# Attention, Fourier mixing and two MLPs: the first chunk's layer norm moved into attention

## The chip, the cores and the metric

The kernel runs on one core of a Trainium2 chip. The metric is the device time of one execution in microseconds (us), lower is better. TensorE is called PE below, VectorE DVE, ScalarE ACT, GpSimd POOL and SyncE SP, as in the profile's rows.

## What is computed

The reference chains three blocks on float32 data. Batch is 4, with 8 heads, a sequence of 576 and a head size of 64, so the model width is 512.

```python
def _attn_ref(q, k, v):
    scores = scale * np.matmul(q, k.transpose(0, 1, 3, 2))
    mask_local = (rel >= 0) & (rel < stride)
    mask_strided = (rel >= 0) & (pos[None, :] % stride == pos[:, None] % stride)
    ...
    attn = softmax(np.where(mask, scores, -1e9))
    return np.matmul(attn, v)

def _moe_ref(x, w_ch1, w_ch2):
    X = np.fft.fft(np.fft.fft(x, axis=1), axis=2)
    u = x + np.real(X)
    un = (u - mean(u)) / np.sqrt(var(u) + 1e-06)
    return u + np.maximum(un @ w_ch1, 0.0) @ w_ch2

def _moe2_ref(x, w_tok1, w_tok2, w_ch1, w_ch2):
    h = np.maximum(x.transpose(0, 2, 1) @ w_tok1, 0.0) @ w_tok2
    u = x + h.transpose(0, 2, 1)
    return u + np.maximum(u @ w_ch1, 0.0) @ w_ch2
```

Half of the heads use the local mask, half the strided one. The change touches the layer norm in the middle of the second block (`un`), for the first 384 of its 2304 rows.

## The kernel before, in words

**Attention.** There are 24 groups, six for each batch element b: three of local heads (kind "l") and three of strided heads (kind "s"). Groups are numbered 0 to 23 by `gno` in the main loop. A group has two halves e = 0 and 1. For each half PE makes the scores `sc` (mask first, then keys), DVE takes a row maximum (`TENSOR_REDUCE st<-sc`), ACT makes four exps `sm<-sc` with their sums, PE transposes them (`tp<-sm`), ACT copies the transposes (`pt<-tp`), PE multiplies with the values (`av<-pt`), and DVE scales (`x<-av`). SP writes `x` to the DRAM tensor `xd[b]`.

**Fourier mixing.** Two or three groups later the Fourier transform of a finished batch element is laid in slices between the groups: SP loads `xa` and `xr` from `xd`, DVE makes `w` and `e`, ACT and POOL split `e` into a high and a low part `f`, PE makes five products `g` in banks of the PSUM tag "m" (two of them), ACT and DVE copy each bank out as `gh` and `gl`, PE makes `fa` and `fb`, and DVE adds the result to `xa` and `xr`, which SP writes to `ud[b]`. The fourth batch element's transform comes after attention, beside the first MLP.

**Layer norm and first MLP.** Rows of `ud` are loaded back as tiles `u` of 128 rows (three tiles are one chunk of 384 rows, called u0, u1, u2 for the first chunk, u3 to u5 for the second). `ln_stats` (lines 452 to 463) takes BN_STATS and BN_AGGR on DVE, a Sqrt on ACT (line 459) and a reciprocal on DVE (line 460), `ln_apply` (lines 465 to 468) makes `lm` on ACT, `Mlp.transposes` (lines 390 to 401) transposes it on PE to `ut` and splits it into `uth` (ACT) and `utl` (DVE). `gemm1` and `gemm2` then run over 16 column blocks, with the products `h` and `oo`.

In the main loop the first chunk is loaded at group 19, its statistics are asked for at group 23 behind the reduce of group 21, and `lm` and the transposes follow after the loop (lines 582 to 606).

**What sets the order.** Tile frees and waits are found by the framework, which also reorders each engine's instructions by a timeline of its own before the program is built. Each engine then runs its list strictly in that order, and SP issues its DMAs in that order, waiting in place for what a DMA depends on. `behind(ins, prev)` asks that `ins` stand behind `prev` in the order, without a wait on the chip. Pools are stacks of memory: the pool "mlp" (`dp`) is opened where "attn" (`ap`) was closed, so that its first tiles overlie `vs`, `qz0`, `qz1`.

Of the kernel before, what the change touches and what calls it, by code (L numbers as in the profile page):

```python
# [9 lines left out]
F32 = mybir.dt.float32  # L10
F32R = mybir.dt.float32r
I32 = mybir.dt.int32
U32 = mybir.dt.uint32
AF = mybir.ActivationFunctionType
ALU = mybir.AluOpType
AX = mybir.AxisListType

B, H, S, D = 4, 8, 576, 64
DM = 512
P = 128  # L20
# [10 lines left out]
SR = [18 * c for c in SC]  # L31


E_MIN = float(np.array(1024 << 20, np.int32).view(np.float32))
E_MAX = float(np.array(1279 << 20, np.int32).view(np.float32))

# [6 lines left out]
def attention_fourier_mlp_kernel(ctx: ExitStack, tc: tile.TileContext, a: dict, out: bass.AP):  # L43
    nc = tc.nc
# [118 lines left out]
    k_t, qz = {}, []  # L163
# [221 lines left out]
    class Mlp:  # L385
# [3 lines left out]

        def transposes(self, c, i, src):  # L390
            if i == 0:
                self.uT[c] = (self.pool.tile([P, 4, 384], F32R, tag="uth", name="uth", bufs=2),
                              self.pool.tile([P, 4, 384], F32R, tag="utl", name="utl", bufs=2))
            th, tl = self.uT[c]
            tp = (ps_o if c < self.split else ps_m)("ut")
            for kd in range(4):
                nc.tensor.transpose(tp[:, kd * P:(kd + 1) * P], src[:, kd * P:(kd + 1) * P], ident)
            tv = tp.rearrange("p (k t) -> p k t", k=4)
            s = slice(i * P, (i + 1) * P)
            nc.scalar.activation(out=th[:, :, s], in_=tv, func=AF.Copy)  # L400
            nc.vector.tensor_tensor(out=tl[:, :, s], in0=tv, in1=f32(th[:, :, s]), op=ALU.subtract)
# [46 lines left out]
    def ln_load(T, mlp):  # L448
        u = mlp.u[T // 3, T % 3] = mlp.u_tile(T // 3)
        return u_rows(T, u)  # L450

    def ln_stats(us, pool, prev=None):
        n = len(us)
        mv = pool.tile([P, 3, 4], F32, tag="mv", name="mv", bufs=2)
        for i, u in enumerate(us):
            st = pool.tile([P, 6], F32, tag="bs", name="bs", bufs=2)
            behind(nc.vector.bn_stats(out=st, in_=u), prev)
            nc.vector.bn_aggr(out=mv[:, i, 0:2], in_=st)
        behind(nc.scalar.activation(out=mv[:, :n, 2], in_=mv[:, :n, 1], func=AF.Sqrt, bias=eps), gl[-1].exp)
        nc.vector.reciprocal(out=mv[:, :n, 3], in_=mv[:, :n, 2])  # L460
        nc.vector.scalar_tensor_tensor(out=mv[:, :n, 2], in0=mv[:, :n, 0], scalar=-1.0, in1=mv[:, :n, 3],
                                       op0=ALU.mult, op1=ALU.mult)
        return [mv[:, i] for i in range(n)]

    def ln_apply(u, mv, pool):
        m = pool.tile([P, DM], F32, tag="lm", name="lm", bufs=2)
        nc.scalar.activation(out=m, in_=u, func=AF.Identity, scale=mv[:, 3:4], bias=mv[:, 2:3])
        return m

    def ln(u, pool):  # L470
# [2 lines left out]
    if True:  # L473
# [14 lines left out]
        nc.vector.memset(eps, 1e-6)  # L488
        nc.scalar.activation(out=warm, in_=eps, func=AF.Exp)
        v_t["s"] = ap.tile([126, 5, 256], F32, name="vs")  # L490
        for g in range(2):
            qz.append(ap.tile([P, 2, 2, S], F32, name=f"qz{g}"))
        v_t["l"] = ap.tile([P, 6, 256], F32, name="vl")
        load_qk(0, 0, ap)
        for g in range(2):
# [59 lines left out]
        def group(g, e, nm):  # L555
            return getattr(gl[min(g, len(gl) - 1)], nm)[e if g < len(gl) else 1]

        slices = []

        for gno, g in enumerate(gl):  # L560
            b, gi = g.b, g.gi
            if gi == 3 and b + 1 < B:
                load_qk(b + 1, 0, ap)
                load_vl(b + 1)
            if gi == 0 and b > 0:
                load_qk(b, 1, ap)
                load_vs(b)
            g.scores()
            for e in range(2):
                g.softmax(e)  # L570
            for e in range(2):
                g.trans(e)
            for e in range(2):
                g.av(e)
                g.out(e)
            if gi == 2 and b > 0:
                for i in range(3):
                    four[b - 1].load(i)
                slices += fft(b - 1)
            while slices and slices[0][0] <= gno:  # L580
                slices.pop(0)[1]()
            if gno == 19:
                us = [u_rows(T, lp.tile([P, DM], F32, tag="u", name="u", bufs=6)) for T in range(3)]
            if gno == 23:
                mvs = ln_stats(us, lp, gl[21].red[1])
            if gno == 9:
                hold[0] = four[0].last
            if gno >= 2 and (gno - 2) % 3 == 0:
                advance()
                load_wa()  # L590
# [12 lines left out]
        for T in range(3):  # L603
            m1.u[0, T] = us[T]
        for T in range(3):
            m1.transposes(0, T, ln_apply(us[T], mvs[T], lp))
        fk["mlp"] = dp
        for i in range(3):
            four[3].load(i)
# [62 lines left out]
        def c_load(b, ts):  # L672
            for t in ts:
# [6 lines left out]
                else:  # L680
                    r = m1.u_tile(0)
                    if t % 3 == 0:
                        for nm in ("uth", "utl"):
                            xbuf[nm] = dp.tile([P, 3, DM], F32R, tag=nm, name=nm, bufs=2)
                    h, l = xbuf["uth"][:, t % 3], xbuf["utl"][:, t % 3]
                q = slice(q0, q0 + n)
                nc.sync.dma_start(out=r[q], in_=x2d[p][j, q, :])
                nc.scalar.activation(out=h[q], in_=r[q], func=AF.Copy)
# [43 lines left out]
        def c1(b):  # L732
# [11 lines left out]
            for m in range(2):  # L744
                if b == 1:
                    if m == 0:
                        th, tl = (dp.tile([P, 3, DM], F32R, tag=nm, name=nm, bufs=2) for nm in ("uth", "utl"))
                    hh, hl = th[:, m], tl[:, m]
                elif b > 1:
                    hh, hl = (wa.tile([P, DM], F32R, tag="wa", name=nm) for nm in ("hh", "hl"))  # L750
                else:
# [432 lines left out]
```

## Time and profile before

| | us |
|---|---|
| median of 3 runs | 936.71 |
| lowest and highest | 935.81, 942.67 |
| the profiled execution | 935.66 |
| its span, first to last instruction | 933.9 |
| PE busy in it | 900.8 (96%) |
| DVE, ACT, POOL busy | 551.6, 411.5, 322.7 |

The profiled execution's own time is 1.76 us longer than its span. Times in rows count from the start of the span. Attention runs to about 149 us; the first MLP starts at about 150 us. Mean granted clock of PE in the execution is 0.99 of 2.4 GHz.

### The profile page before, as it was taken

What the parts mean: (1) busy time and instruction counts of PE and PEld (TensorE: products, weight loads), DVE (VectorE), ACT (ScalarE), POOL (GpSimd) and SP (SyncE); (2) the same over time, 40 slices, a digit from 0 to 9 for tenths busy, and PEclk for the clock granted to TensorE, in tenths of its full rate; (3) what the DMA queues carried; (4) which work ended last, traced back from release to release, by engine and by line L of the source; (5) the groups of instructions that cost most, each with busy time, mean ns of one, the idle gap of its engine ahead of it and who ended that gap; (6) DMA issues with size and microseconds to landing.
All of it is one profiled execution on the core that took longest, in us unless ns stands there. A gap on an engine that the chain in (4) does not pass through costs nothing.

```text
span 933.9 us, 15390 instructions
## 1 busy us (share of the span) xinstructions
PE 900.8 (96%) x5554; PEld 831.1 (89%) x5554; DVE 551.6 (59%) x1022; ACT 411.5 (44%) x1073; POOL 322.7 (35%) x378
## 2 busy tenths in 40 slices
PE   6979998999999999999999998999999999999997
PEld 5869997999899889888888987777899999999997
DVE  4758876988884433444443444735534444888774
ACT  4978768453342234233323333323445445454432
POOL 2402202333320143344444345622223001946660
PEclk9889999999999999999999999999999999999999
DMA  9988772434331254544754665588833287146351
GB/s 244 277 266 246 222 229 89 153 114 147 131 111 66 82 171 128 192 126 140 213 149 133 206 183 166 171 271 287 318 127 146 102 270 228 44 160 215 132 196 46
DMA packets 116915, 161.00 MB, mean 172 GB/s; under 512 B 9602, under 2 KB 70120, under 8 KB 116840
## 3 DMA queue, kind: packets, MB, share of 16 engines
q1 hardware_dynamic: 114872, 157.30, 53.4%
q0 software_dynamic: 1712, 2.51, 1.1%
q8 instruction: 44, 0.72, 0.3%
q14 instruction: 31, 0.25, 0.1%
q10 hardware_dynamic: 256, 0.21, 0.1%
HBM read 104.93 MB, written 55.06 MB: 171 GB/s over the span
## 4 chain that ended last, share of the span: by engine, by line
PE 56%; DMA 9%; DVE 7%; SPq 4%; ACT 3%; POOL 3%; issue 2%; DVEq 0%; ACTq 0%; POOLq 0%
PE oo L994 14%; PE oo L430 10%; PE h L411 10%; PE z L853 8%; PE y L853 4%; DMA wraw<-in_w1b_dram 4%; PE tk L742 3%; SPq L102 3%; PE tu L764 2%; PE w L853 2%; POOL wt L148 2%; DVE wu L113 2%; DMA wraw<-in_w2b_dram 2%; DVE wu L114 1%; ACT wu L107 1%
## 5 line engine op out<-in xcount | busy, mean ns | idle before, releaser
L994 PE MATMUL oo<-wo,ht 128*128 128x256 f32 x972 | 135.2, 281 | 0.0
L411 PE MATMUL h<-uth,wAh 128*128 128x384 f32 x384 | 130.0, 339 | 0.0
L411 PE MATMUL h<-uth,wAl 128*128 128x384 f32 x384 | 129.5, 337 | 0.0
L411 PE MATMUL h<-utl,wAh 128*128 128x384 f32 x384 | 129.5, 337 | 0.0
L994 PEld LDWEIGHTS oo<-wo,ht 128*128 128x128 f32 x972 | 127.5, 188 | 0.0
L430 PE MATMUL oo<-wAh,hh 128*128 128x512 f32 x288 | 114.0, 398 | 3.6 <-ACT hh L415 3.6
L430 PE MATMUL oo<-wAl,hh 128*128 128x512 f32 x288 | 113.6, 395 | 0.0
L430 PE MATMUL oo<-wAh,hl 128*128 128x512 f32 x288 | 104.8, 396 | 2.9 <-DVE hl L416 2.8
L416 DVE SCALAR_TENSOR_TENSOR hl<-h,hh 128x384 fp32r<-128x384 f32 x96 | 52.6, 552 | 78.4 <-ACT hh L415 78.4
L125 POOL TENSOR_TENSOR wAl<-wu,wAh 128x512 fp32r<-128x512 f32 x32 | 46.0, 1441 | 94.5 <-ACT wAh L124 90.5
L109 DVE TENSOR_SCALAR wu<-wu 128x512 f32<-128x512 f32 x56 | 29.4, 525 | 82.9 <-ACT wu L107 74.9
L148 POOL TENSOR_TENSOR wt<-wu 128x128 f32<-128x128 f32 x48 | 21.1, 460 | 161.0 <-DVE wu L114 157.8
L415 ACT ACTIVATE hh<-h 128x384 fp32r<-128x384 f32 x96 | 45.7, 484 | 67.3 <-PE h L411 67.2
L411 PEld LDWEIGHTS h<-uth,wAl 128*128 128x128 f32 x384 | 72.2, 188 | 3.0
L411 PEld LDWEIGHTS h<-utl,wAh 128*128 128x128 f32 x384 | 72.2, 188 | 2.1
L411 PEld LDWEIGHTS h<-uth,wAh 128*128 128x128 f32 x384 | 72.1, 188 | 2.2
L107 ACT ACTIVATE wu<-wraw 128x512 f32<-128x512 f32 (+1 forms) x62 | 40.8, 660 | 74.9 <-DMA wraw<-in_w1b_dram 45.7
L430 PEld LDWEIGHTS oo<-wAh,hl 128*128 128x128 f32 x288 | 53.8, 188 | 17.5 <-DVE hl L416 5.5
L430 PEld LDWEIGHTS oo<-wAh,hh 128*128 128x128 f32 x288 | 54.1, 188 | 14.7 <-ACT hh L415 5.2
L853 PE MATMUL z<-ut,wo 128*128 128x384 f32 x324 | 65.1, 340 | 1.4 <-DVE ut L821 1.4
L430 PEld LDWEIGHTS oo<-wAl,hh 128*128 128x128 f32 x288 | 54.1, 188 | 8.8
L229 ACT ACTIVATE sm<-sc,st 96x128 f32<-96x128 f32 (+2 forms) x176 | 61.3, 362 | 0.6
(198 smaller groups left out, 1966.6 us busy)
## 6 DMA issues: line engine op xcount, KB each, us to landing
wo<-wsd SPq DMA_DIRECT2D x84, 256.0 KB
wsd<-wbh SPq DMA_DIRECT2D x24, 448.0 KB
wsd<-wbl SPq DMA_DIRECT2D x24, 448.0 KB
u<-u2d SPq DMA_DIRECT2D x36, 256.0 KB
hd<-hs SPq DMA_DIRECT2D x12, 768.0 KB
hw<-hd SPq DMA_DIRECT2D x36, 256.0 KB
wraw<-in_w1a_dram SPq DMA_DIRECT2D x16, 512.0 KB
wraw<-in_w2a_dram SPq DMA_DIRECT2D x16, 512.0 KB
```

Source lines behind the costliest of these rows:

```text
L102: behind(nc.sync.dma_start(out=raw[:, n:n + w], in_=src.rearrange("p (c t) -> p c t", t=2)), hold[0])
L107: behind(nc.scalar.activation(out=f32(u), in_=f32(high), func=AF.Abs, scale=2.0**16), relu.get("hh"))
L109: clamp = eng().tensor_scalar(f32(u), f32(u), E_MIN, E_MAX, op0=ALU.max, op1=ALU.min)
L125: nc.gpsimd.tensor_tensor(out=lo[:, :n], in0=u, in1=f32(hi[:, :n]), op=ALU.subtract)
L148: nc.gpsimd.tensor_tensor(out=o, in0=x, in1=y, op=ALU.add if plus else ALU.subtract)
L229: self.exp = nc.scalar.activation(out=smv[:, j, :], in_=sc[:, j, :], func=AF.Exp, scale=SCALE, bias=st[:, 1, j:j + 1], accum_out=st[:, 2, ...
L411: nc.tensor.matmul(out=h[:, :384], lhsT=l[:, ws], rhs=r[:, kd, :], start=x == 0, stop=x == 11)
L415: relu["hh"] = nc.scalar.activation(out=hh, in_=h[:, :384], func=AF.Relu)
L416: relu["hl"] = nc.vector.scalar_tensor_tensor(out=hl, in0=h[:, :384], scalar=0.0, in1=f32(hh), op0=ALU.max, op1=ALU.subtract)
L430: nc.tensor.matmul(out=self.o[c][i], lhsT=l[:, s], rhs=r, start=first and x == 0, stop=last and x == 2)
L853: Unit.last = nc.tensor.matmul(out=bank[:, :384], lhsT=w[:, c + kd * P:c + kd * P + P], rhs=r[:, kd], start=first and x == 0, stop=x == 5, ...
L994: nc.tensor.matmul(out=acc[G][bank][:, 256 * half:256 * half + 256], lhsT=lh[:, i], rhs=w[:, c:c + 256], start=m == 0 and x == 0 and half ...
```

## The change

Five edits. The first chunk's rows are loaded at group 15 and not 19, and the statistics are asked for at group 17, behind that group's own reduce, and not at group 23. The statistics of several tiles at once take their inverse root by Newton's steps on DVE (`inverse_root`, a start value from the bits of the number, then three steps), and those of a single tile still by ACT's Sqrt. `lm` of u0 and u1 is made at groups 18 and 19, behind that group's last exp; that of u2 stays after the loop. The two buffers `qz0` and `qz1` are allocated in the other order. `uth` and `utl` become one tile `uT` with two halves, at each place that uses them.

```diff
+SEED = -0.67709067 * 2.0**-65
...
         def transposes(self, c, i, src):
             if i == 0:
-                self.uT[c] = (self.pool.tile([P, 4, 384], F32R, tag="uth", name="uth", bufs=2),
-                              self.pool.tile([P, 4, 384], F32R, tag="utl", name="utl", bufs=2))
+                t = self.pool.tile([P, 2, 4, 384], F32R, tag="ut", name="uT", bufs=2)
+                self.uT[c] = t[:, 0], t[:, 1]
...
+    def inverse_root(y, var, pool):
+        n = var.shape[1]
+        t = pool.tile([P, 2, 4], F32, tag="nr", name="nr", bufs=1)
+        v, z = t[:, 0, :n], t[:, 1, :n]
+        nc.vector.tensor_scalar_add(v, var, 1e-6)
+        nc.vector.tensor_scalar(z.bitcast(I32), v.bitcast(I32), 1, -1, op0=ALU.logical_shift_right, op1=ALU.bitwise_xor)
+        nc.vector.tensor_scalar_mul(y, z, SEED)
+        for _ in range(3):
+            nc.vector.scalar_tensor_tensor(out=z, in0=y, scalar=-0.5, in1=v, op0=ALU.mult, op1=ALU.mult)
+            nc.vector.tensor_tensor(out=z, in0=z, in1=y, op=ALU.mult)
+            nc.vector.scalar_tensor_tensor(out=y, in0=z, scalar=1.5, in1=y, op0=ALU.add, op1=ALU.mult)
...
-        behind(nc.scalar.activation(out=mv[:, :n, 2], in_=mv[:, :n, 1], func=AF.Sqrt, bias=eps), gl[-1].exp)
-        nc.vector.reciprocal(out=mv[:, :n, 3], in_=mv[:, :n, 2])
+        if n > 1:
+            inverse_root(mv[:, :n, 3], mv[:, :n, 1], pool)
+        else:
+            behind(nc.scalar.activation(out=mv[:, :n, 2], in_=mv[:, :n, 1], func=AF.Sqrt, bias=eps), gl[-1].exp)
+            nc.vector.reciprocal(out=mv[:, :n, 3], in_=mv[:, :n, 2])
...
-    def ln_apply(u, mv, pool):
+    def ln_apply(u, mv, pool, prev=None):
         m = pool.tile([P, DM], F32, tag="lm", name="lm", bufs=2)
-        nc.scalar.activation(out=m, in_=u, func=AF.Identity, scale=mv[:, 3:4], bias=mv[:, 2:3])
+        behind(nc.scalar.activation(out=m, in_=u, func=AF.Identity, scale=mv[:, 3:4], bias=mv[:, 2:3]), prev)
...
-        for g in range(2):
-            qz.append(ap.tile([P, 2, 2, S], F32, name=f"qz{g}"))
+        qz += [ap.tile([P, 2, 2, S], F32, name=f"qz{g}") for g in (1, 0)][::-1]
...
-            if gno == 19:
+            if gno == 15:
                 us = [u_rows(T, lp.tile([P, DM], F32, tag="u", name="u", bufs=6)) for T in range(3)]
-            if gno == 23:
-                mvs = ln_stats(us, lp, gl[21].red[1])
+            if gno == 17:
+                mvs = ln_stats(us, lp, g.red[1])
+            if 18 <= gno < 20:
+                ln1.append(ln_apply(us[gno - 18], mvs[gno - 18], lp, g.exp))
...
-            m1.transposes(0, T, ln_apply(us[T], mvs[T], lp))
+            m1.transposes(0, T, ln1[T] if T < 2 else ln_apply(us[T], mvs[T], lp))
```

Nothing is added to or taken from PE's, POOL's and SP's work; DVE has eleven instructions more, ACT one less. The order of the instructions is another on DVE, ACT and PE from about group 18 to the middle of the first MLP, and the same before and behind that. Three places, with the buffers' numbers behind the names:

On DVE, before, from the first reduce of group 18 (`st_1505<-sc_1492`) to the first reduce of group 19 (`st_1588`); `gl` copies a Fourier bank `g` out:

```order
L226 TENSOR_REDUCE st_1505<-sc_1492 96x4
L261 TENSOR_SCALAR st_1416<-st_1416 108x4
L262 RECIPROCAL st_1416<-st_1416 108x4
L263 TENSOR_TENSOR x_1383<-av_1374,st_1346 108x512
L342 TENSOR_TENSOR gl_1458<-g_1447,gh_1457 128x290
L226 TENSOR_REDUCE st_1505<-sc_1498 96x4
L342 TENSOR_TENSOR gl_1472<-g_1461,gh_1471 128x290
L226 TENSOR_REDUCE st_1588<-sc_1575 96x4
```

The same place in the changed kernel, where `st_1535` is group 18's, `u_1335` is u1 and `u_1337` is u2:

```order
L470 BN_STATS bs_1485<-u_1335 128x6
L471 BN_AGGR mv_1481<-bs_1482 128x2
L227 TENSOR_REDUCE st_1535<-sc_1522 96x4
L262 TENSOR_SCALAR st_1422<-st_1422 108x4
L471 BN_AGGR mv_1481<-bs_1485 128x2
L264 TENSOR_TENSOR x_1389<-av_1380,st_1352 108x512
L263 RECIPROCAL st_1422<-st_1422 108x4
L343 TENSOR_TENSOR gl_1464<-g_1453,gh_1463 128x290
L227 TENSOR_REDUCE st_1535<-sc_1528 96x4
L470 BN_STATS bs_1488<-u_1337 128x6
L343 TENSOR_TENSOR gl_1478<-g_1467,gh_1477 128x290
L264 TENSOR_TENSOR x_1447<-av_1442,st_1422 108x256
```

BN_STATS of u1 stands ahead of group 18's first reduce now, and that of u2 between its second reduce and the second `gl`; one BN_AGGR later comes group 19's first reduce, then Newton's steps, and BN_STATS of u3 ahead of the last of them.

On SP, before, the writes of the last rows of the first batch element to `ud0`, the queries and keys of the last batch element's strided heads, and the load of u2 (`u_1668`):

```order
L373 DMA ud0_73<-xr_713 33x512
L374 DMA ud0_73<-xa_712 32x512
L176 DMA qz1_137<-in_qt_dram 64x1152
L177 DMA k_1487<-in_kt_dram 128x1152
L445 DMA u_1668<-ud0_73 128x512
L276 DMA xd2_71<-x_1383 9x6x256
```

The same place in the changed kernel, with u2 as `u_1337`:

```order
L375 DMA ud0_73<-xa_712 32x512
L374 DMA ud0_73<-xr_713 33x512
L177 DMA qz1_136<-in_qt_dram 64x1152
L446 DMA u_1337<-ud0_73 128x512
L178 DMA k_1517<-in_kt_dram 128x1152
L277 DMA xd2_71<-x_1389 9x6x256
```

The two writes have changed places, and the load of u2 stands ahead of the keys' load and not behind it.

On ACT, before, from group 19's first exps (`sm_1587`) to the start of its second half (`st_1588<-st_1588`):

```order
L229 ACTIVATE sm_1587,st_1588<-sc_1575,st_1588 96x128 x4
L340 ACTIVATE gh_1557<-g_1547 128x290
L340 ACTIVATE gh_1571<-g_1561 128x290
L239 ACTIVATE pt_1531<-tp_1526 128x384
L239 ACTIVATE pt_1607<-tp_1602 128x384
L227 ACTIVATE st_1588<-st_1588 96x4
```

The same place in the changed kernel, where `lm_1605` is the layer norm of u0:

```order
L230 ACTIVATE sm_1619,st_1620<-sc_1607,st_1620 96x128 x3
L341 ACTIVATE gh_1587<-g_1577 128x290
L230 ACTIVATE sm_1619,st_1620<-sc_1607,st_1620 96x128
L240 ACTIVATE pt_1561<-tp_1556 128x384
L483 ACTIVATE lm_1605<-u_1333,mv_1481 128x512
L341 ACTIVATE gh_1601<-g_1591 128x290
L240 ACTIVATE pt_1639<-tp_1634 128x384
L228 ACTIVATE st_1620<-st_1620 96x4
```

`lm` of u0 stands ahead of a Fourier copy `gh`, of group 19's first `pt` and of its second half. The load of ACT's table for Sqrt stands behind the last exp of attention in both kernels, ahead of a Sqrt of three columns and one of a single column before, of one of a single column (u3's) now.

## Rows read from the trace of the kernel before

**Rows 1.** Stretches: length, busy (instructions) of PE, PEld, DVE, ACT, POOL; clock, DMA, GB/s.

```profile
116.00:126.00 10.00, 10.00 (x94) 9.55 (x93) 4.22 (x11) 7.61 (x38) 0.52 (x1) 1.00 0.75 243
126.00:140.00 14.00, 14.00 (x134) 13.74 (x132) 12.89 (x30) 8.99 (x40) 1.81 (x2) 1.00 0.68 224
140.00:150.00 10.00, 7.38 (x54) 5.67 (x53) 8.52 (x29) 9.06 (x38) 2.03 (x3) 1.00 0.21 60
```

**Rows 2.** Timeline of PE, 140 to 150 us.

```profile
140.56 1.30 PE L237 MATMUL tp<-ident_r,sm 108*108 108x108 f32 x4 [0.24 <-ACT sm L229]
...
148.18 0.97 PE L252 MATMUL av<-vs,pt 108*108 108x64 f32 x8 [1.43 <-ACT pt L239]
...
149.86 0.85 PE L332 MATMUL g<-cs,f 128*128 128x290 f32 x4 [0.71 <-ACT f L315]
```

**Rows 3.** Timeline of ACT, the same stretch.

```profile
146.11 1.28 ACT L459 ACT_TABLE_LOAD   x1
...
149.71 1.51 ACT L467 ACTIVATE lm<-u,mv 128x512 f32<-128x512 f32 x2
```

**Rows 4.** Timeline of DVE, 136 to 140 us.

```profile
138.02 1.27 DVE L457 BATCH_NORM_STATS2 bs<-u 128x6 f32<-128x512 f32 x2
139.22 0.58 DVE L226 TENSOR_REDUCE st<-sc 108x4 f32<-108x432 f32 x1
```

**Rows 5.** Stretches of 2 us, PE alone.

```profile
148.00:150.00 2.00, 1.11 (x9) 1.00 0.22 64
150.00:152.00 2.00, 2.00 (x11) 0.62 0.28 83
152.00:154.00 2.00, 2.00 (x11) 0.53 0.19 56
```

**Rows 6.** Timeline of SP, 108 to 122 us: issues and waits.

```profile
109.51 0.32 SPq L445 DMA_DIRECT2D u<-ud  x1
...
113.23 0.43 SPq L373 DMA_DIRECT2D ud<-xr  x1
113.70 0.34 SPq L374 DMA_DIRECT2D ud<-xa  x1
...
114.72 1.44 SPq L177 DMA_DIRECT2D k<-in_kt_dram  x1
...
116.94 0.34 SPq L445 DMA_DIRECT2D u<-ud  x1
...
120.58 0.46 SPq L445 DMA_DIRECT2D u<-ud  x1
```

**Rows 7.** Timelines of SP and DVE: a load of u4's half, its use.

```profile
143.88 0.49 SPq L445 DMA_DIRECT2D u<-ud  x1
...
147.08 1.29 DVE L457 BATCH_NORM_STATS2 bs<-u 128x6 f32<-128x512 f32 x2 [1.06 <-DMA u<-ud]
```

**Rows 8.** Timeline of DVE, 110 to 118 us.

```profile
110.71 0.67 DVE L226 TENSOR_REDUCE st<-sc 96x4 f32<-96x512 f32 x1
...
114.33 0.68 DVE L226 TENSOR_REDUCE st<-sc 96x4 f32<-96x512 f32 x1
114.93 0.44 DVE L342 TENSOR_TENSOR gl<-g,gh 128x290 fp32r<-128x290 f32 x1
115.30 0.68 DVE L226 TENSOR_REDUCE st<-sc 96x4 f32<-96x512 f32 x1
...
116.81 0.17 DVE L261 TENSOR_SCALAR st<-st 96x8 f32<-96x8 f32 x1 [0.50 <-ACT sm L229]
```

**Rows 9.** The page's groups of instructions: the exps.

```profile
L229 ACT ACTIVATE sm<-sc,st 96x128 f32<-96x128 f32 (+2 forms) x176 | 61.3, 362 | 0.6
```

**Rows 10.** Timeline of PE, 114 to 118 us.

```profile
114.83 0.50 PE L237 MATMUL tp<-ident_r,sm 96*128 96x96 f32 x4
115.12 1.86 PE L332 MATMUL g<-ss,f 128*128 128x290 f32 x12
116.85 0.65 PE L332 MATMUL g<-ss,f 128*128 128x290 f32 x3
```

More of the change, by code (lines that the diff above doesn't have):

```diff
@@ L556, in group @@
             return getattr(gl[min(g, len(gl) - 1)], nm)[e if g < len(gl) else 1]
-        slices = []
+        slices, ln1 = [], []
         for gno, g in enumerate(gl):
@@ L682, in c_load @@
                     if t % 3 == 0:
-                        for nm in ("uth", "utl"):
-                            xbuf[nm] = dp.tile([P, 3, DM], F32R, tag=nm, name=nm, bufs=2)
-                    h, l = xbuf["uth"][:, t % 3], xbuf["utl"][:, t % 3]
+                        xbuf["t"] = dp.tile([P, 2, 3, DM], F32R, tag="ut", name="uT", bufs=2)
+                    h, l = xbuf["t"][:, 0, t % 3], xbuf["t"][:, 1, t % 3]
                 q = slice(q0, q0 + n)
@@ L746, in c1 @@
                     if m == 0:
-                        th, tl = (dp.tile([P, 3, DM], F32R, tag=nm, name=nm, bufs=2) for nm in ("uth", "utl"))
-                    hh, hl = th[:, m], tl[:, m]
+                        t = dp.tile([P, 2, 3, DM], F32R, tag="ut", name="uT", bufs=2)
+                    hh, hl = t[:, 0, m], t[:, 1, m]
                 elif b > 1:
```

## The prediction

> **What bounds the kernel now.** Read the table of stretches first: TensorE (PE) is busy for the whole of 116 to 140 us, and in 140 to 150 us for 7.38 of 10 us [rows 1]; from 150 us on it is full again [rows 5]. So in this part of the program only an idle us of PE, or a us at the lower clock, is worth anything. Where the idle time lies is read from PE's timeline: 1.43 us before an `av` that waited for ACT's copy `pt`, 0.71 us before a `g` that waited for ACT's `f` [rows 2]. In the same rows the four transposes at 140.56 took 1.30 us, where four of the kind take 0.50 [rows 10]: 0.8 us more of waiting, hidden in the modelled ends. Then the clock: after those gaps the grant reads 0.62 and 0.53 for two stretches of 2 us, in which PE is full [rows 5]. That is the 1.2 GHz level for part of them, and costs (1 - 0.62) x 2 + (1 - 0.53) x 2 = 1.70 us.
>
> Why ACT is late at the end of attention: it loads a table there (1.28 us) and applies the layer norm (1.51 us for two tiles) [rows 3], and before that it waited for group 22's reduce, which stood on VectorE (DVE) behind two BN_STATS; these began at 138.02, the reduce at 139.22 [rows 4]. This is the end that the change lightens. All that can come back there is 2.62 + 1.70 + 0.8 = 5.1 us.
>
> **What goes from the end.** BN_STATS of the tiles u0 to u3 (two of them 1.27 us [rows 4], so 0.64 each, 2.5 us in all) leave DVE in 133 to 140, so the reduce of group 22 can start up to 1.2 us sooner. Two of the first chunk's three ACT `lm` (0.75 each) leave ACT's last stretch. The Sqrt of three columns goes, but the table load does not: the first Sqrt of a single tile now stands at the same place, behind the last exp. So Newton's steps save one short ACT instruction, not the 1.28 us.
>
> **What comes in the middle.** Here a wait is added: the statistics now stand on DVE among groups 17 to 19, and DVE runs its list in order. What a load takes is seen where DVE waited for one: issued 143.88, released 147.08, 3.2 us [rows 7]. That was a load of 128 KB, the nearest row; these are 256 KB.
>
> u1 is issued at 109.51 [rows 6], so it is there at 112.7; with 0.64 of BN_STATS and a short BN_AGGR the first reduce of group 18 starts at 113.4 instead of 110.71 [rows 8]. In the trace the four exps behind it (0.362 us each [rows 9]) are done at about 111.4 + 0.3 + 1.45 = 113.1, and PE asks for them at 114.83 [rows 10], so 1.7 of the 2.7 us is cover. PE loses 1.0 us.
>
> u2 costs most. SP issues its load only when the write of `xa` to `ud0` has landed: 113.70 to 116.94, 3.24 us [rows 6]. The change puts this write in front of `xr`'s, at 113.23, so the load goes out at 113.23 + 3.24 = 116.5 and is there at 119.7. DVE reaches BN_STATS of u2 at about 115.8 (the second reduce of group 18 in its place at 114.33 [rows 8], moved by 0.8, and its 0.68) and stands still for 3.9 us. Behind it wait `gl` (0.44), an `x`, and the reduce of group 19, which began at 115.30 [rows 8]. PE needs `gl` to free a bank for the fourth `g` slice, which it reaches at 116.85 [rows 10] + 1.0 = 117.85; `gl` is done at 119.7 + 0.64 + 0.44 = 120.8. PE loses 2.9 us. Bounds: if the load were there when DVE comes, nothing; if it took 1.5 longer, 4.4. I take 2.9, from the nearest rows.
>
> Group 19's reduce starts at about 121.1 (after `gl`, `x` and BN_AGGR), and its four exps with a `gh` between them end at 121.1 + 0.68 + 0.3 + 1.45 + 0.35 = 123.9. PE has about 2.2 us of its own list from 120.8 (nine `g` at 1.86 / 12 = 0.155 [rows 10], eight short `av`), so it loses a further 0.8 us.
>
> u3: SP now has the `k` load (1.44) between u2 and the four `xd` writes, and `vs` before u3. In the trace u3 went out 120.58 - 116.94 = 3.64 after u2 [rows 6]; now at 116.5 + 3.64 + 1.44 + 0.45 = 122.0, there at 125.2. Newton's thirteen dependent short steps at 0.20 each (one at 116.81 is busy for 0.17 [rows 8], and the next must be started) are 2.6 us, and end before that: the wait for u3 covers them; without it they would cost about 2 us at this place. BN_STATS of u3 stands ahead of the last step, so ACT's first `lm` starts at 126.1 and holds the `gh` and `pt` behind it until 127.2. PE has some 3.0 us of work from 123.9 and then waits for the bank that `gl` frees at 127.6 (0.7 us), and for the next exps, done at 129.3 (0.5 us). I take 1.2 us, an estimate from these sums; 0 if u3 is there in time, 2.7 if it too is 1.5 later.
>
> **Clock.** PE idle for 2.9 us at 118 to 121 is no less than what stood before the fall at 150 (2.0 - 1.11 in 148 to 150 [rows 5], and the 1.43 [rows 2]). I charge half of that fall, 0.85 us, because the waits for group 19 and u3 lie in the same microseconds and hide the rest; bounds 0 and 1.70.
>
> **At nothing.** `lm` moved into attention is 1.5 us of ACT where it is busy for 8.99 of 14 us [rows 1]; if that cover were gone, 1.5 us. The one tile for both halves adds no instruction and the order of the two `qz` buffers only changes what later tiles overlie: 0, within 0.5 either way. From about 160 us DVE is tight and the order of its work on the last Fourier batch is changed too; 0, within 0.7.
>
> **Sum.** Lost: 1.0 + 2.9 + 0.8 + 1.2 + 0.85 = 6.75 us. Returned: a PE that is late by that much finds its copies ready at the end of attention, so the 5.1 us of gaps and low clock there go. Net +1.65 us on the profiled execution's 935.66 us: 937.3 us. The median of the runs shown is 936.71, 1.05 above that execution, so this is a small loss or nothing; 1% (9.4 us) is about what a measurement of this kernel can tell from no change.
>
> A rule of the Trainium skill gives another price for the loads: in "DMA: Bandwidth & Descriptors", section "Anatomy of one DMA — SWDGE (gpsimd) path", a transfer is a fixed 2.0 us and its bytes at 436 GB/s. By it the write of 64 KB and the load of 256 KB together would take 2.15 + 2.6 us, u2 would be there at 118.0, PE would lose 1.7 us less, and the time would be an estimated 935.6. It is written for POOL's queue, these loads come from SP's, and the wait of rows 7 took 3.2 us where it gives 2.3, so I stay with the row.
>
> **Rivals.**
> A. The loads are there when DVE comes, and only the gain is left. For it: the load of u1 was issued early, and DVE is busy for only 4.22 of 10 us in 116 to 126 [rows 1]. Against it: u2's issue cannot come before the write has landed [rows 6], 2 us after DVE reaches its place. Time: 935.66 - 5.1 + 1.0 = 931.6.
> B. Slower: the loads of u2 and u3 each land 1.5 us later than reckoned (the DMA engines are busy for 0.75 of 116 to 126 us [rows 1], and a `k` of 576 KB goes between them), so both waits grow by that; the whole fall of the clock is paid; and ACT, held by `lm` at 126 us, stays late to the end, so the 5.1 us do not return. Time: 935.66 + 6.75 + 3.0 + 0.85 = 946.3. It decides from the point where PE still stands idle in the last 10 us of attention although it came there late. Against it: ACT has idle time in 126 to 140 to catch up [rows 1].
> C. Newton's steps free ACT of the table load and bring their 1.28 us: excluded, since a Sqrt with its load stands at the same place.
>
> **Chances.** Forecast 0.68, for itself 934 to 940.5; A 0.24; B 0.08. The range reaches down into A and stops above the forecast's own upper end: 930.8 to 943.5. Slower by over 1% needs most of B: 0.04; faster by over 1% needs more than all of A: 0.02; within 1%: 0.94.
>
> **What would show it.** Right, if in the changed profile DVE waits 3 to 5 us for `u<-ud` near 116 us, PE stands 2 to 4 us before a `g` <- `ss` near 118 us, the second table load is there near the end of attention, and PE has no gap between the last `av` and the first `ut`. Wrong, if DVE meets u2 without a wait (then A), or if PE is idle for 2 us or more in the last 10 us of attention (then B).

## The result, and the profile after

| | before | after |
|---|---|---|
| median of 20 runs each, us | 936.34 | 944.32 |
| lowest and highest | 932.94, 942.67 | 937.97, 947.64 |
| the profiled execution | 935.66 | 945.24 |
| its span | 933.9 | 943.5 |

The ratio is 1.0085, with a 95% interval of 1.0071 to 1.0100: the changed kernel is slower by some 8 us. The forecast was 937.3 with a range up to 943.5, so the time lies above it: the direction was named rightly, but the loss is five times as large.

The table of stretches of the changed kernel, to be read against [rows 1], with one stretch more (length, busy us and instructions of PE, PEld, DVE, ACT, POOL; granted clock, DMA share, GB/s):

```profile
116.00:126.00 10.00, 8.35 (x70) 7.45 (x69) 4.39 (x20) 4.79 (x24) 0.14 (x1) 1.00 0.83 249
126.00:140.00 14.00, 11.14 (x100) 10.50 (x99) 8.80 (x22) 10.40 (x46) 0.52 (x1) 1.00 0.42 141
140.00:150.00 10.00, 9.46 (x90) 9.10 (x89) 10.00 (x26) 8.10 (x35) 2.74 (x3) 1.00 0.44 133
150.00:160.00 10.00, 7.94 (x60) 6.76 (x60) 6.74 (x24) 9.00 (x26) 3.05 (x2) 1.00 0.24 72
```

Where PE was full before, in 116 to 140 us, it now lacks 1.65 + 2.86 us. Attention now ends at 154.6 us; in the two stretches around that point PE still lacks 0.54 + 2.06 us. The rows of PE's timeline that stand behind a gap (start, busy us, engine, line, what; in brackets the idle time and what ended it) answer to [rows 2]; the last two are in the first MLP:

```profile
120.14 0.40 PE L333 MATMUL g<-ss,f 128*128 128x290 f32 x1 [1.48 <-DVE gl L343]
...
130.03 0.51 PE L359 MATMUL fa<-cd,gh 128*128 128x258 f32 x2 [2.86 <-DVE gl L343]
...
146.93 0.40 PE L333 MATMUL g<-cs,f 128*128 128x290 f32 x1 [0.54 <-POOL f L317]
...
153.66 0.97 PE L253 MATMUL av<-vs,pt 108*108 108x64 f32 x8 [1.13 <-ACT pt L240]
...
158.18 2.69 PE L333 MATMUL g<-ss,f 128*128 128x290 f32 x18 [0.86 <-DVE gl L343]
...
169.73 0.50 PE L431 MATMUL oo<-wAh,hh 128*128 128x512 f32 x1 [0.80 <-DVE uT L402]
...
175.56 0.50 PE L431 MATMUL oo<-wAh,hh 128*128 128x512 f32 x1 [0.75 <-DVE uT L402]
```

DVE's timeline shows the three waits for loads that the change put into the middle, to be read beside [rows 4] and [rows 8], and that for u4 at the end:

```profile
112.64 0.69 DVE L470 BATCH_NORM_STATS2 bs<-u 128x6 f32<-128x512 f32 x1 [1.02 <-DMA u<-ud]
...
119.03 0.69 DVE L470 BATCH_NORM_STATS2 bs<-u 128x6 f32<-128x512 f32 x1 [2.84 <-DMA u<-ud]
...
127.37 0.69 DVE L470 BATCH_NORM_STATS2 bs<-u 128x6 f32<-128x512 f32 x1 [3.81 <-DMA u<-ud]
...
152.62 0.69 DVE L470 BATCH_NORM_STATS2 bs<-u 128x6 f32<-128x512 f32 x1 [1.89 <-DMA u<-ud]
```

SP's timeline shows when the loads were issued, as [rows 6] do for before, and ACT's that the table load still stands ahead of the last copies ([rows 3]):

```profile
113.80 0.40 SPq L375 DMA_DIRECT2D ud<-xa  x1
...
115.55 0.35 SPq L446 DMA_DIRECT2D u<-ud  x1
115.95 0.42 SPq L178 DMA_DIRECT2D k<-in_kt_dram  x1
...
119.69 0.42 SPq L184 DMA_DIRECT2D vs<-in_vs_dram  x1
120.16 0.37 SPq L446 DMA_DIRECT2D u<-ud  x1
```

```profile
151.78 1.28 ACT L475 ACT_TABLE_LOAD   x1
...
155.27 1.51 ACT L483 ACTIVATE lm<-u,mv 128x512 f32<-128x512 f32 x2
```

The last 10 us of attention, up to the end of the last `av`, in the kernel before and in the changed one (length, PE busy and instructions, granted clock, DMA share, GB/s):

```profile
139.15:149.15 10.00, 8.09 (x61) 1.00 0.19 54
```

```profile
144.63:154.63 10.00, 8.27 (x76) 1.00 0.22 67
```

PE is idle for 1.91 us there before and for 1.73 us after.

**A stretch that can be compared.** PE's list of before is that of after too up to the middle of attention, and again from a point in the first MLP on. Single executions differ by several us outside the changed part: the 281st matmul that writes `sc` (group 16) starts anywhere from 92.7 to 101.3 us. So each execution below is also measured from that matmul over the 329th that writes `av` (the first of group 22) to the 346th that writes `h` (in the first MLP, some 290 us), all counted in PE's timeline. In between, PE's order differs from kernel to kernel, but at each of these three points every kernel below has issued the same matmuls, so the parts can be compared. The first part holds the middle of attention, the second its end and what follows.

| us | group 16 to 22 | 22 to first MLP | together | median of runs, and of before beside it |
|---|---|---|---|---|
| before | 46.4 | 148.4 | 194.8 | 936.3 |
| before once more | 47.3 | 148.2 | 195.6 | |
| after | 51.4 | 149.2 | 200.7 | 944.3, 936.3 |
| after once more | 53.4 | 149.7 | 203.2 | |
| buffers | 46.8 | 148.2 | 195.1 | 933.8, 935.4 |
| u2_wait | 48.9 | 148.1 | 197.0 | 938.4, 936.3 |
| before_table | 46.6 | 148.4 | 195.0 | 935.0, 935.3 |
| u3_late | 48.3 | 151.9 | 200.2 | 940.3, 935.4 |
| u3_early | 50.2 | 147.5 | 197.7 | 942.4, 935.4 |
| stats_20 | 46.0 | 155.9 | 201.9 | 943.5, 935.4 |
| stats_19b | 45.3 | 149.7 | 195.0 | 936.5, 936.3 |
| stats_19b_table | 46.5 | 149.9 | 196.4 | 938.6, 935.3 |
| stats_19b_table_u45 | 45.6 | 148.7 | 194.3 | 936.4, 935.3 |
| u3_late_newton_all | 50.0 | 162.0 | 212.1 | 954.0, 936.3 |

The two lines of after against the two of before: 4.1 to 7.1 us are lost in the middle, and nothing comes back behind it; a further 0.8 to 1.5 us are lost there. Together that is 5.1 to 8.4 us of the 8. The loss in the middle is PE's idle time and its clock: the gaps of the first part add up to 0.5 us in both executions of before, to 5.0 us in after, and to 4.2 us in after once more, which lost 3.4 us to the clock as well. Medians of the experiments are over 12 runs where the text says nothing else (7 of stats_20, 6 of u3_late_newton_all); the two second profiles are single executions and have none.

### The profile page after: what moved, and what is told of

It is laid out like the page before. It is cut to its first block, busy times and chain, and to the rows that moved or that the text cites. A ratio compares the mean times of both kernels' runs of the same rounds, so it can differ in the third digit from the quotient of the medians.

```text
span 943.5 us, 15393 instructions
## 1 busy us (share of the span) xinstructions
PE 905.9 (96%) x5554; PEld 834.6 (88%) x5554; DVE 556.9 (59%) x1033; ACT 410.3 (43%) x1072; POOL 319.8 (34%) x378
## 4 chain that ended last, share of the span: by engine, by line
PE 51%; DMA 10%; DVE 8%; SPq 4%; POOL 4%; ACT 3%; issue 3%; DVEq 0%; ACTq 0%; POOLq 0%
PE oo L1010 14%; PE oo L431 8%; PE z L869 8%; PE h L412 7%; DMA wraw<-in_w1b_dram 5%; PE y L869 4%; SPq L103 3%; PE tk L758 3%; POOL wt L149 3%; PE tu L780 3%; DVE wu L114 2%; PE w L869 2%; DMA wraw<-in_w2b_dram 2%; DVE wu L115 2%; ACT wu L108 2%
## 5 line engine op out<-in xcount | busy, mean ns | idle before, releaser
L412 PE MATMUL h<-uT,wAh 128*128 128x384 f32 x768 | 203.5, 339 | 0.0
L412 PEld LDWEIGHTS h<-uT,wAh 128*128 128x128 f32 x768 | 139.4, 188 | 4.8
L412 PE MATMUL h<-uT,wAl 128*128 128x384 f32 x384 | 129.5, 337 | 0.0
L416 ACT ACTIVATE hh<-h 128x384 fp32r<-128x384 f32 x96 | 45.6, 484 | 73.1 <-PE h L412 73.0
L126 POOL TENSOR_TENSOR wAl<-wu,wAh 128x512 fp32r<-128x512 f32 x32 | 42.2, 1323 | 97.3 <-ACT wAh L125 92.1
L412 PEld LDWEIGHTS h<-uT,wAl 128*128 128x128 f32 x384 | 72.1, 188 | 3.0
L108 ACT ACTIVATE wu<-wraw 128x512 f32<-128x512 f32 (+1 forms) x62 | 40.9, 662 | 71.7 <-DMA wraw<-in_w1b_dram 48.9
L869 PEld LDWEIGHTS z<-ut,wo 128*128 128x128 f32 x324 | 57.1, 188 | 2.1 <-DVE ut L837 2.0
L114 DVE SCALAR_TENSOR_TENSOR wu<-wraw,wu 128x512 int32<-128x512 int32 (+1 forms) x62 | 54.5, 879 | 1.1
```

The lines of the kernel that those rows point to most:

```text
L108: behind(nc.scalar.activation(out=f32(u), in_=f32(high), func=AF.Abs, scale=2.0**16), relu.get("hh"))
L114: v.scalar_tensor_tensor(out=u, in0=high, scalar=-2**31, in1=u, op0=ALU.bitwise_and, op1=ALU.bitwise_or)
L126: nc.gpsimd.tensor_tensor(out=lo[:, :n], in0=u, in1=f32(hi[:, :n]), op=ALU.subtract)
L412: nc.tensor.matmul(out=h[:, :384], lhsT=l[:, ws], rhs=r[:, kd, :], start=x == 0, stop=x == 11)
L416: relu["hh"] = nc.scalar.activation(out=hh, in_=h[:, :384], func=AF.Relu)
L869: Unit.last = nc.tensor.matmul(out=bank[:, :384], lhsT=w[:, c + kd * P:c + kd * P + P], rhs=r[:, kd], start=first and x == 0, stop=x == 5, ...
```

## The experiments

Three theories stood at the start. W: PE loses its time behind DVE's waits for the loads of u2 and u3. E: what is lost is lost at the end of attention and behind it. B: the order of the buffers and the single tile cost it. Within the stretch of the table, E holds for 0.8 to 1.5 us at most. The diffs say which kernel they are made on.

### The second profiles: after_again and before_again

No edit.

> The changed kernel once more, for a second profile: which of its gaps come again. By every theory the waits for u2 and u3 do, 1.3 to 1.7 us and 2.6 to 3.1 us on PE; the stretch from 300 to 590 us, whose list of instructions is that of the kernel before, shows how much of a difference of 2 us there is chance.

> The kernel before once more, for a second profile: its gaps of 1.43 and 0.71 us at the end of attention should come again; whether the low clock behind them (1.70 us) does too is open, since the runs of other kernels show it after gaps of like size in one and not in another.

after_again, one execution: 948.3 us. PE's waits for u2 and u3 came again, 1.64 and 2.04 us, and so did the one before the last `av`, 1.11 us; the second is shorter than the 2.6 to 3.1 us that were expected. The rows of PE, and stretches of 4 us (length, PE busy, granted clock, DMA share, GB/s):

```profile
120.24 0.40 PE L333 MATMUL g<-ss,f 128*128 128x290 f32 x1 [1.64 <-DVE gl L343]
...
130.48 0.50 PE L359 MATMUL fa<-cd,gh 128*128 128x258 f32 x2 [2.04 <-DVE gl L343]
```

```profile
120.00:124.00 4.00, 3.76 (x26) 0.73 0.89 255
124.00:128.00 4.00, 4.00 (x32) 0.84 0.35 109
...
132.00:136.00 4.00, 4.00 (x22) 0.57 0.37 127
```

Here the clock fell behind the gaps: (1 - 0.73) x 4 + (1 - 0.84) x 4 + (1 - 0.57) x 4 = 3.4 us in 120 to 136 us. In the first profile the same gaps left it at 1.00. That is about as much as the two executions differ by (3.1 us).

before_again, one execution: 939.1 us. The waits at the end of attention are there again, 1.43 and 0.96 us, with a clock of 0.83 over 150 to 160 us:

```profile
151.34 0.97 PE L252 MATMUL av<-vs,pt 108*108 108x64 f32 x8 [1.43 <-ACT pt L239]
...
153.27 1.15 PE L332 MATMUL g<-cs,f 128*128 128x290 f32 x4 [0.96 <-ACT f L315]
```

How much is chance where PE's list is the same: from the 346th to the last `h` of the first MLP (about 300 to 590 us) the two executions of before take 294.1 and 296.3 us, those of after 296.4 and 296.1 us. So a difference of 2 us there says nothing.

### buffers

```diff
-            if gno == 15:
+            if gno == 19:
...
-            if gno == 17:
-                mvs = ln_stats(us, lp, g.red[1])
-            if 18 <= gno < 20:
-                ln1.append(ln_apply(us[gno - 18], mvs[gno - 18], lp, g.exp))
+            if gno == 23:
+                mvs = ln_stats(us, lp, gl[21].red[1])
```

(against after; `lm` and the Sqrt as in before too)

> Only the buffers are changed: the two halves as one tile, the two qz in the other order; the layer norm (load at group 19, statistics at 23, Sqrt) is that of the kernel before. Theories W and E: 936.3 within 1 us. Rival B: 940 or more. The first MLP, from 160 to 600 us, shows whether the tile in one piece makes PE wait more there: 2 us or more by B, under 0.5 us by the others.

Measured: 933.84 us, ratio 0.9990 (0.9963 to 1.0018), and 195.1 us in the compared stretch. The buffers cost nothing; theory B falls.

### u3_late

```diff
-            m1.transposes(1, T - 3, ln(ln_load(T, m1), lp))
+            m1.transposes(1, T - 3, ln(ln_load(T, m1), lp, gl[21].red[1]))
```

(against after; `ln` hands the last argument on to `ln_stats` as `prev`)

> BN_STATS of u3, u4 and u5 stand behind the reduce of group 21 again, all else is as in the changed kernel. Theory W (PE loses its time behind DVE's waits for loads): DVE no longer stands 3.81 us for u3 ahead of Newton's last step, PE's wait of 2.86 us before fa <- cd goes, a part of it comes back as a shorter return, and the time falls by 1.5 to 3 us, to 941.3 to 942.8. The wait of 1.48 us before g <- ss (for u2) stays. Rival E (what is lost is lost at the end of attention and in the first steps of the MLP, and a gap in the middle is paid back there): the time stays within 1 us of 944.3. Rival B (the order of the buffers and the single tile cost it): 944.3 too.

Measured: 940.26 us, ratio 1.0046 (1.0025 to 1.0067). The wait of 2.86 us is gone, that for u2 stays:

```profile
123.93 0.40 PE L333 MATMUL g<-ss,f 128*128 128x290 f32 x1 [1.18 <-DVE gl L343]
```

By the ratios, (1.0085 - 1.0046) x 936 = 3.7 us came back, somewhat more than W expected; the two intervals do not overlap. In its profiled execution the compared stretch is hardly shorter than in after, but that is the clock behind the end of attention, in three stretches of 4 us:

```profile
156.00:160.00 4.00, 2.64 (x13) 0.50 0.25 76
160.00:164.00 4.00, 3.25 (x14) 0.50 0.36 97
164.00:168.00 4.00, 4.00 (x25) 0.78 0.73 242
```

(1 - 0.50) x 4 twice and (1 - 0.78) x 4 are 4.9 us. Without them the stretch would be 195.3 us (both profiles of before hold 1.7 us of such loss).

### u3_early

```diff
-                us = [u_rows(T, lp.tile([P, DM], F32, tag="u", name="u", bufs=6)) for T in range(3)]
+                us = [u_rows(T, lp.tile([P, DM], F32, tag="u", name="u", bufs=6)) for T in range(4)]
```

(against after; the statistics still take the first three, and the MLP takes the fourth as its u3)

> u3 is loaded straight behind u2, ahead of the loads of k and vs; its BN_STATS stays early. If u3 came late (7.2 us from issue to use) because 630 KB of vs and 576 KB of k stood ahead of it in the queue: u3 is used within 5 us of its issue, DVE waits for it under 2 us behind u2, PE's wait before fa <- cd falls from 2.86 to under 1 us, the one before g <- ss may grow by up to 1 us, and the time falls by 1 to 3 us, to 941 to 943. If the load is slow whatever stands ahead of it: 7 us again, DVE waits 3 us or more, and the time stays at 944 or rises.

Measured: 942.36 us, ratio 1.0065 (1.0040 to 1.0090), 197.7 us in the compared stretch. SP issues both loads in one row of 0.83 us, and DVE uses u2 3.7 us and u3 5.7 us after the row began:

```profile
110.69 0.83 SPq L446 DMA_DIRECT2D u<-ud  x2
...
114.77 0.46 SPq L178 DMA_DIRECT2D k<-in_kt_dram  x1
```

```profile
114.35 0.70 DVE L470 BATCH_NORM_STATS2 bs<-u 128x6 f32<-128x512 f32 x1 [2.96 <-DMA u<-ud]
...
116.42 0.69 DVE L470 BATCH_NORM_STATS2 bs<-u 128x6 f32<-128x512 f32 x1 [1.01 <-DMA u<-ud]
```

The second of the two, issued about 0.4 us into the row, took some 5.3 us behind one load of 256 KB; in after u3 took 7.2 us behind k and vs. DVE's second wait is 1.01 us in place of 3.81, and the wait before `fa` is gone. So the expectation on the queue holds in the main: 5.3 us is a little over the 5 that it allowed. A wait of 1.61 us before `g` stays, that for u2. By the medians the gain over after is 2 us, and the two intervals overlap; the stretch is 3.0 us shorter than in the first profile of after.

### stats_20

```diff
-            if gno == 17:
+            if gno == 20:
                 mvs = ln_stats(us, lp, g.red[1])
-            if 18 <= gno < 20:
-                ln1.append(ln_apply(us[gno - 18], mvs[gno - 18], lp, g.exp))
+            if 21 <= gno < 23:
+                ln1.append(ln_apply(us[gno - 21], mvs[gno - 21], lp, g.exp))
```

(against after, with the edit of u3_late)

> The first chunk is loaded at group 15 as in the changed kernel, but its statistics are asked for at group 20, behind that group's reduce, its lm at groups 21 and 22, and BN_STATS of u3 to u5 behind the reduce of group 21: by then every load has long landed. Theory W: DVE waits for no load up to 145 us, PE has no gap over 0.3 us from 110 to 140 us, and the time falls to that of the kernel before or below it, 932 to 937. Rival E: the end of attention loses as it does in the changed kernel, 941 to 943. Rival B: 944.

Measured: 943.46 us, ratio 1.0090 (1.0057 to 1.0123). W in its plain form fails: no load is waited for, PE has no gap from 110 to 140 us, the stretch from group 16 to 22 takes 46.0 us (46.4 in before), and yet the time is that of after. It is lost behind that (155.9 us in place of 148.4). DVE, ACT and PE:

```profile
135.38 0.14 DVE L457 TENSOR_SCALAR nr<-mv 128x3 f32<-128x3 f32 x1
...
150.74 0.14 DVE L477 SCALAR_TENSOR_TENSOR mv<-mv 128x3 f32<-128x3 f32 x1
```

```profile
150.92 1.52 ACT L483 ACTIVATE lm<-u,mv 128x512 f32<-128x512 f32 x2 [0.18 <-DVE mv L477]
```

```profile
151.31 4.72 PE L333 MATMUL g<-ss,f 128*128 128x290 f32 x18 [1.19 <-DVE gl L343]
155.82 1.62 PE L398 MATMUL ut<-ident_r,lm 128*128 128x128 f32 x8
```

The steps of Newton's method stand among the fullest work of DVE. Back to back they were reckoned at 2.6 us, and here they take from 135.4 to 150.7 us. `lm` of u0 and u1 follows at 150.9, behind attention, and PE, which has run its `g` at half the clock (granted 0.50; 18 products in 4.72 us, 2.69 us in after at 1.00), comes to the first `ut` at 155.8; in before it was 150.6. This run shows that something else costs beside the waits for loads, and led to the next. What it is in detail is not shown: PE's rows name DVE's `gl` (1.19 us) and the copies `pt` and `f`, and not `lm`, so the steps may cost by `lm` being late or by what they hold up on DVE.

### stats_19b

As stats_20, with `if gno == 19` in place of 20; `lm` stays at groups 21 and 22.

> As stats_20, but the first chunk's statistics are asked for at group 19, behind its second reduce, and lm at groups 21 and 22; BN_STATS of u3 to u5 behind the reduce of group 21. In stats_20 no load was waited for, but Newton's steps lay in the fullest stretch of DVE and took from 135.4 to 150.7 us, so that lm came after attention. Here they lie among groups 20 and 21, where DVE has idle time. Theory W2 (two things cost: DVE's waits for loads, and a layer norm that is ready too late for the transposes behind attention): neither is there, Newton's steps take under 10 us, PE has no gap over 0.3 us from 110 to 140 us, the time is 934 to 937.5. Rival E (something at the end of attention that every version with Newton has, such as the table load in front of the last copies): 940 to 943.

Measured: 936.46 us, ratio 1.0002 (0.9981 to 1.0022): the whole loss of after is gone in the sum. BN_STATS of u2 waits for nothing, and Newton's steps end at 129.5:

```profile
121.19 0.66 DVE L470 BATCH_NORM_STATS2 bs<-u 128x6 f32<-128x512 f32 x1
...
129.39 0.11 DVE L477 SCALAR_TENSOR_TENSOR mv<-mv 128x3 f32<-128x3 f32 x1
```

PE has no gap from 110 to 140 us. The steps take 6.4 us (from 122.9), and not 15. The kernel differs from stats_20 in nothing but the place of the statistics, so this shows the core of theory W2: the change loses by where the statistics stand, and not by Newton's steps or `lm` as such. It also shows that little is to be gained: the change is then as fast as before within 0.2%. By the table it gains 1.0 to 2.0 us up to group 22 and loses 1.3 to 1.4 us behind it, where PE waits 1.50 us for the last `pt`.

### u2_wait

```diff
-            if gno == 19:
+            if gno == 15:
                 us = ...
+            if gno == 17:
+                junk = lp.tile([P, 6], F32, tag="bs", name="bs", bufs=2)
+                behind(nc.vector.bn_stats(out=junk, in_=us[2]), g.red[1])
```

(against before)

> The kernel before, with two edits: the first chunk is loaded at group 15, and DVE takes one BN_STATS of u2 (its result is used by nothing) behind group 17's reduce; the statistics that count stay at group 23. PE's list is that of the kernel before up to the second MLP (some 586 us). So DVE stands still for u2 in the middle of attention, and nothing else is moved. DVE should wait 2 to 4 us there, and PE lose 1 to 3 us near 120 us. By the step of the prediction that a PE which comes late finds its copies ready: PE's waits at the end of attention (1.43 and 0.71 us) shrink by as much, and the stretch from 100 to 300 us is as long as before within 0.8 us. By theory S (the copies at the end are started by PE's own scores, so they come late with it): those waits stay as they are within 0.3 us, what PE lost stays lost, and the time is 937.3 to 939.3.

Measured: 938.43 us, ratio 1.0020 (0.9997 to 1.0044). DVE stood 4.19 us for u2, and PE 1.62 us:

```profile
120.09 0.36 SPq L445 DMA_DIRECT2D u<-ud  x1
```

```profile
125.47 0.69 DVE L586 BATCH_NORM_STATS2 bs<-u 128x6 f32<-128x512 f32 x1 [4.19 <-DMA u<-ud]
```

```profile
126.85 0.56 PE L332 MATMUL g<-cs,f 128*2 128x290 f32 x3 [1.62 <-DVE gl L342]
...
154.43 0.97 PE L252 MATMUL av<-vs,pt 108*108 108x64 f32 x8 [1.44 <-ACT pt L239]
...
156.03 1.33 PE L332 MATMUL g<-cs,f 128*128 128x290 f32 x4 [0.63 <-ACT f L315]
```

The waits at the end are 1.44 and 0.63 us, where they were 1.43 and 0.71 with a PE that came 1.6 us earlier. The compared stretch is 1.4 to 2.2 us longer than in the two profiles of before: 1.5 to 2.5 us are lost up to group 22, and the part behind is 0.1 to 0.3 us shorter. So theory S holds in the profile: what PE loses in the middle does not shorten its waits at the end. The median agrees (2.2 us more), though its interval does not exclude no change.

### before_table

```diff
-            nc.scalar.activation(out=pt[:k, :nt * q], in_=tp[:k, :nt * q], func=AF.Copy)
+            self.copy = nc.scalar.activation(out=pt[:k, :nt * q], in_=tp[:k, :nt * q], func=AF.Copy)
...
-func=AF.Sqrt, bias=eps), gl[-1].exp)
+func=AF.Sqrt, bias=eps), gl[-1].copy)
```

(against before)

> The kernel before with one edit: ACT's load of the table for Sqrt, and the two Sqrt, stand behind the last two copies pt of attention and not behind the last exp; PE's list is the same. If the load in front of the copies is what holds the end of attention: PE's wait of 1.43 us before the last av falls under 0.3 us, nothing takes its place, and the time is 934 to 935. If the copies are only the first of two things that are late (the f behind it waits for DVE, whose BN_STATS wait for u4): the wait before the last av goes, the one before g <- cs grows from 0.71 to about 2 us, and the time stays within 0.7 us of 936.3.

Measured: 935.01 us, ratio 0.9999 (0.9979 to 1.0018). The second expectation came true: the wait before `av` is gone, and the next one has grown from 0.71 to 1.84 us:

```profile
147.58 0.80 PE L332 MATMUL g<-cs,f 128*128 128x290 f32 x4 [1.84 <-ACT f L315]
```

### stats_19b_table and stats_19b_table_u45

The edit of before_table on stats_19b; in the second, BN_STATS of u4 and u5 stand behind the last group's `x` as well.

> stats_19b with the same edit. There the eight transposes ut stand between the last av and the g that needs f, so a part is kept: PE's wait of 1.50 us before the last av goes, a new one of 0.5 to 1 us before g <- cs comes, 935.3 to 936.3. If the table load alone held the end: 934.5 to 935.

> As stats_19b_table, and BN_STATS of u4 and u5 (for which DVE waited 2.34 us for a load in stats_19b) stand behind the last x of attention, so the second thing that is late is gone too: no wait over 0.4 us before the last av and before g <- cs, 933.5 to 935. If something else holds PE there (the copies gh and gl behind the exps): 935.5 to 936.5.

Measured: 938.61 us, ratio 1.0026 (1.0009 to 1.0044), and 936.43 us, ratio 1.0004 (0.9986 to 1.0023). The first lies above both of its expectations, by 2.3 us or more; in place of its wait before `av`, PE now waits 1.01 us for DVE's `x` before the transposes `ut`, and why the whole is slower than stats_19b was not settled. The second gives its second number, that of something else that holds PE: the wait before `av` is gone, the one before `g` is 0.65 us, and 0.86 us for `gl` before the next `g` remain:

```profile
147.64 0.81 PE L333 MATMUL g<-cs,f 128*128 128x290 f32 x4 [0.65 <-ACT f L316]
...
150.42 2.68 PE L333 MATMUL g<-ss,f 128*128 128x290 f32 x18 [0.86 <-DVE gl L343]
```

Its compared stretch is the shortest of all, 194.3 us, by 0.5 to 1.3 us against before; the runs can't tell it from before. No version tried is shown to be faster than the kernel before.

### u3_late_newton_all

In `ln_stats` the branch on `n` goes and every tile takes `inverse_root` (against u3_late).

> As u3_late, and the single tiles take Newton's steps too, so ACT loads no table for Sqrt (and none for anything else from 150 us on). If the table load of 1.28 us still sets the end of attention: PE's wait before the last av goes, and the time falls by 1 to 2 us from u3_late, to 938.3 to 939.3. If what it frees on ACT is taken on DVE (three tiles by 13 steps of 0.16 to 0.2 us, 6.2 to 7.8 us, before 180 us, where DVE is full): 940 to 944.

Measured: 954.00 us, ratio 1.0175 (1.0145 to 1.0205), far beyond both expectations. The table load is gone, but PE stands for DVE:

```profile
153.97 1.09 PE L398 MATMUL ut<-ident_r,lm 128*128 128x128 f32 x4 [2.63 <-DVE nr L462]
...
179.70 0.51 PE L359 MATMUL fb<-sd,gh 128*128 128x258 f32 x2 [4.09 <-DVE m L367]
```

Against u3_late that is some 12 us by the ratios. The sum of the steps (6.2 to 7.8 us for three tiles) was expected to be the price. The rows show that `lm` and the Fourier sum `m` are late as well, and the clock fell: the 18 products `g` at 157.65 take 4.72 us (granted 0.50). My reading is that a chain of dependent steps lies between other work in a full list, as in stats_20, and holds up all that stands behind it; no run takes this apart.

## Why the prediction was wrong

**The step that failed** is in the sum: "Returned: a PE that is late by that much finds its copies ready at the end of attention, so the 5.1 us of gaps and low clock there go." Nothing came back: behind group 22 the two profiles of after take 0.8 to 1.5 us more than those of before, and in the last 10 us of attention PE is idle for 1.73 us in place of 1.91. In after PE still waits 0.54, 1.13 and 0.86 us at the end of attention, and 0.80 and 0.75 us behind it. The low clock (1.7 us in both profiles of before) is gone in after and there again in after_again. u2_wait shows the same with PE's list unchanged: with a PE that came 1.6 us later the waits at the end are 1.44 and 0.63 us, where they were 1.43 and 0.71. My reading of it: the exps, the table load and the copies of the last groups are started by PE's own scores, so they are late with it; the prediction treated them as work with a time of its own.

**The losses in the middle** were forecast at 6.75 us; the two profiles of after lose 4.1 to 7.1 us against those of before from group 16 to 22. That the sum is near is in part luck, for its terms were off in both directions:

- u1: its reduce was to start at 113.4 and started at 113.33. PE was to lose 1.0 us, and its timeline shows no gap there; its list at this place is another one, with products `sc` between the transposes.
- u2: the write took 1.75 us from issue to the load's issue (113.80 to 115.55; 1.71 in u2_wait), not the 3.24 of [rows 6], in which SP's issue of `k` (1.44 us) lies as well, so the load was issued at 115.55 and not 116.5. The load itself took 3.5 us (3.2 reckoned). DVE waited 2.84 us (3.9), PE 1.48 us (2.9), and the 0.8 us behind it were 0.17. The rule of the Trainium skill ("DMA: Bandwidth & Descriptors", section "Anatomy of one DMA — SWDGE (gpsimd) path") gives an estimated 2.15 and 2.6 us for these two; it is stated for POOL's queue. The write was shorter than that and the load longer, so neither it nor the row fits both; in the sum, 5.2 us were measured, where the rule gives 4.75 and the rows 6.44.
- u3: reckoned to be there at 125.2, it was used at 127.37, though it was issued 1.8 us earlier than reckoned. I counted the time that SP needs to issue `k` and `vs`, and not their 576 and 630 KB, which go out ahead of u3 in its queue (`k` 4.2 us and `vs` 0.5 us earlier; how much of `k` was still to be moved is not shown). It took 7.2 us. PE lost 2.86 us in place of 1.2, and by the medians of u3_late this wait is worth about 3.7 us of the whole.
- The clock: 0.85 us were charged. It cost 0 in the one profile of after and 3.4 us in the other.

**The signs.** Of the four signs of being right, two came: the table load near the end, and no gap between the last `av` and the first `ut`. DVE's wait for u2 (2.84 us, where 3 to 5 were named) and PE's before `g` (1.48 us, where 2 to 4 were named) fell short. The sign for B, 2 us idle in the last 10 us of attention, was set too high to tell: it read 1.73, and 1.91 in before.

**The rivals.** B (946.3, chance 0.08) named the sign of what happened: "PE still stands idle in the last 10 us of attention although it came there late". Its number is the nearest of the three, but its reason is not the one shown: it made `lm` on ACT hold the end up, and u2_wait has no `lm` in the middle and returns no more. Of its two late loads, u3 came 2.2 us later than reckoned, and u2 0.7 us earlier. A is excluded: DVE met u2 without its load. C was rightly excluded, the table load stands where it stood; and u3_late_newton_all shows that taking it away in that manner costs some 12 us.

**At nothing.** The buffers: right, 0.9990. The order of DVE's work from about 160 us on was put at 0, within 0.7: too little. PE waits there for DVE's `uT` before two `oo`, 0.80 and 0.75 us in after, 0.24 and 0.75 us in after_again, and in neither profile of before. buffers, which has the single tile too, has no such wait, so the tile alone does not make it.

**What stays open.** The compared stretch holds 5.1 to 8.4 us of the loss of 8; the single profiles do not narrow that down. From the 346th `h` to the end the two profiles of after take 644.9 and 645.4 us and those of before 641.9 and 642.4, though PE's list is the same there. The other kernels lie between 641.4 and 646.1, u3_early highest and stats_20 among the lowest, so no rule that ties this to the change was found; it was not tried further.

## What to carry to other kernels

A wait that was put into the middle of a full engine's work was paid in full here: gaps that stand later need not shrink for it where the work that ends them is itself started by that engine. Before comparing two parts of a timeline, make sure that the same instructions lie in each, for an engine's order may have changed. Before an instruction that needs a load is moved ahead in an engine that runs its list in order, add up the bytes that the queue moves ahead of that load, and not only the issues. And a chain of many short dependent steps belongs into a stretch where its engine is idle: in a full one 13 steps took 15 us, in a quieter one 6.4, and in after the first 12 took 2.6.

## What the runs showed of the hardware

- A load of 256 KB on SP's queue took from issue to use 3.5 us ahead of `k` and `vs` (after, u2), 3.7 us in the same place (u3_late, u2: 119.18 to 122.83), each some 0.9 us behind the issue of `qz` of 288 KB, about 5.3 us behind another load of 256 KB (u3_early, u3), 5.4 us behind `k` of 576 KB (u2_wait, u2: 120.09 to 125.47), and 7.2 us behind `k` and `vs` (after, u3). The Trainium skill says in "DMA: Bandwidth & Descriptors", section "Two DMAs through the same engine are not ordered", that within one queue of one DMA engine descriptors start in order; these times agree with that.
- Gaps of like size at one place of the same program left the granted clock at 1.00 in one execution and cost 3.4 us in another (after and after_again); at the end of attention it cost 1.7 us in before, 4.9 us in u3_late, and nothing in the profile of buffers.
